# Last w_down forms written in place, M's rows on SP's queue, and four steps of the first half's end put elsewhere

## The chip, the cores and the metric

The kernel runs on one core of one Trainium2 chip. Its time is the device time of one execution, in microseconds (us); what is compared is the median of several executions. The core has five instruction streams that run side by side and wait for each other by semaphores: PE (TensorE, matrix products), ACT (ScalarE), DVE (VectorE), POOL (GpSimd) and SP (SyncE). SP computes nothing here and only starts DMA transfers; POOL starts the others. Each of these two streams starts its transfers in the order of its program, and a transfer that must wait for data holds up all that stand behind it in the same stream.

## The reference

```python
x = A_x                                         # 1 x 2048 x 640
g = sigmoid((x * gate_w).sum(-1, keepdims=True))
# a: linear attention, 32 heads of 20
q, k, v = split(x @ wqkv);  pq, pk = phi(q), phi(k)   # phi(t) = (t+1 if t>0 else exp(t)) + 1e-6
kv = einsum("bhsd,bhse->bhde", pk, v);  z = pk.sum(over s)
a = (einsum("bhqd,bhde->bhqe", pq, kv) / (pq . z + 1e-6)) @ wo
# b: GLU, F = 1536
b = (sigmoid(x @ w_gate) * (x @ w_up)) @ w_down
out = g * a + (1 - g) * b
```

All data are fp32.

## The kernel before

**Products.** `mm3` (L406) makes every product of three matmuls, high by high, high by low and low by high: L407, L408 and L409 in the profile's rows. `split` (L437) makes the two parts of an operand: ACT copies it to the reduced type (the high part, L420), and DVE subtracts that copy from the operand (the low part, L424). Large products are done in a 2 by 2 block form that needs fewer block products and more sums and differences of blocks. Tiles called `xah`, `xrh`, `xbh`, `xth`, `b12h` (and `..l` for low) are parts of such combinations of x's blocks; `w`, `wg`, `wu`, `ws`, `wf`, `wd`, `ds` hold weights and combinations of weights; `cc`, `ch`, `dd`, `rot` are names of PSUM buffers, used in turn.

**Stages.** The positions are worked on in two halves, `pr` = 1 first and then 0.
- The K stage (about 4.6 to 145 us) makes k and phi(k) in four chunks and, in batches, `gt`, the product of phi(k) and x. In its loop over chunks (c = 1 to 3, L1080) a table says after which of a block's steps `s1` to `s5` a piece of work called "qw" is run. At c = 3 "qw" is what `queue_ls` (L743) queued: the sums of w_down's blocks for the last pair of F blocks in the tile `qraw` (DVE, in place), and four `form` calls that split them into tiles `qp` and store these in DRAM (`wd_dram`, stores `wd<-qp`). After the loop the pools that hold `qraw` and `qp` are closed, and the tile `xz` (new positions of x, 5 and 3 rows of blocks, two loads `xz<-xt`) lies over the same memory: its loads wait until the stores have read their tiles.
- `q_phase(1)`, `f_phase(1)` and `last_pair(1)` (145 to 406 us): q, the GLU's blocks in pairs, and for each pair `down_pair`, the product with w_down. The result is summed into `tb`. `last_pair` runs the last of these. In `down_pair` the names are PSUM sums: `W`, `X0`, `X1` are new products; a seed (`V`, `Y0`, `Y1`, `R0`, `U0` and so on) is a copy on ACT of one PSUM sum into another buffer, where more products are added; `out` adds a finished sum to `tb` on DVE. The sigmoid of the pair's last block is `tail[4]` (ACT, the row `cx<-cx`).
- `last_stores` holds two stores of 640 KB, `wd<-wd` on POOL: forms of w_down that the second half loads again.
- `q_phase(0)`, `f_phase(0)`, `last_pair(0)` (406 to 660 us): the same for the second half, with most forms loaded again from DRAM. Beside them the denominators and factors of a are worked out, and `load_ms` (L2463) loads raw rows of the matrix M (the heads' kv times wo, `m_dram`) into the tile `mt`: 8 loads, of 80 KB each. A second call loads 8 others into `mr` and `mv`. `load_m` loads the already split M (`mp_dram`) into `ws` and `wf`.
- The A stage (660 to 725 us): phi(q) times M, scaled, added to b's part and stored. `mt` is first read by DVE here.

**What sets the order.** The class `Order` plans while the program is written: it estimates when PE, ACT and DVE will reach each instruction, holds small pieces of work in a list and writes one when it fits ahead of PE (`fill`), when it is due (`need`, as `order.need((nx[1], 2))`) or at a named place (`run("qw")`). `Ring` estimates the two DMA streams, `sp` and `gp` (SP and POOL), and these estimates decide some of the order too. So a step that is moved by hand can also move pieces that the diff doesn't touch. A hook such as `{7: [queue_scaled]}` runs a function after that step of a phase.

Of the kernel before, what the change touches and what calls it, by code (L numbers as in the profile page):

```python
# [8 lines left out]
F32R = mybir.dt.float32r  # L9
# [5 lines left out]
P = 128  # L15
S, D, F = 2048, 640, 1536
# [14 lines left out]
class Order:  # L31
# [267 lines left out]
    def seed(self, out, at):  # L299
        if out is not None and out.tensor._space == PSUM:  # L300
            self.seeded[out.tensor.name] = at
# [73 lines left out]
def gated_mix_kernel(ctx: ExitStack, tc: tile.TileContext, xt, xn, wk, wv, wo, wst_q, wst_f, out_t):  # L375
# [6 lines left out]
    order = Order()  # L382
    rings = Rings()
    sp, gp = Ring(nc.sync, order, rings, 0, 0.38, 1.5), Ring(nc.gpsimd, order, rings, 1, 0.55, 2.2)

    def f32(ap):
        return ap.bitcast(F32)
# [49 lines left out]
    def split(hi, lo, src, after=""):  # L437
        act(hi, src, AF.Copy, after)
        at = order.act + A_LAG

        def low():
            order.vec = max(order.vec, at)
            vec2(lo, src, f32(hi), OP.subtract)
        order.then(low)
# [295 lines left out]
    qs = qs_cm.__enter__()  # L740
    w_dram, wd_dram = {}, {}

    def queue_ls():  # L743

        p, w = FC // 2 - 1, 4 * P
        wd_dram[p] = dram.tile([P, 2, WF], F32, name=f"wd{p}")
        raw = qs.tile([P, 2, D], F32, name="qraw", tag="qraw")[:, :, :w]
        for j in range(2):
            sp.dma_start(raw[:, j], wst_f[2 * p + j, :, 2, :w])
        (a11, a21), (a12, a22) = [raw[:, j].rearrange("p (q h c) -> h p q c", q=2, h=2) for j in range(2)]  # L750

        def sums(part):
            if part == 0:
                add(a22, a21, a22)
                sub(a21, a11, a21)
            else:
                sub(a11, a22, a11)
                sub(a12, a12, a11)

        def form(j, q):  # L760
            cs = slice(j * w + 2 * q * P, j * w + 2 * (q + 1) * P)
            t = qs.tile([P, 2, 2 * P], F32R, name="qp", tag="qp", bufs=2)
            split(t[:, 0], t[:, 1], raw[:, j, 2 * q * P:2 * (q + 1) * P])
            order.then(lambda: gp.dma_start(wd_dram[p][:, :, 2 * D + cs.start:2 * D + cs.stop], f32(t)))
        for part in range(2):
            order.add(0, 2 * v_cost(2 * P), lambda part=part: sums(part), "qw", None, kept=True)
        for j in range(2):
            for q in range(2):
                order.add(a_cost(2 * P), v_cost(2 * P), lambda j=j, q=q: form(j, q), "qw", None, kept=True)
# [249 lines left out]
    c0 = chunks[0]  # L1019
# [61 lines left out]
    for c in range(1, 4):  # L1081
# [4 lines left out]
        for n in range(1, 6):  # L1086
            order.need((ck, n))
            if c == 1 and n >= 3:
                order.need(("ks", (1, 0, 2)[n - 3]))
            getattr(a, f"s{n}")()  # L1090
            getattr(b, f"s{n}")()
            for _ in range(({1: 1, 2: 1, 3: 1, 5: 1}, {3: 2, 4: 1, 5: 1})[c - 2].get(n, 0) if c > 1 else 0):
                order.run("qw")
        order.need((ck, 6))
        if c == 1:
# [495 lines left out]
    last_stores = []  # L1591
# [102 lines left out]
    c_h, c_l = {}, {}  # L1694
# [9 lines left out]
    def m_rows(dst, cols, queue, u=None):  # L1704

        for d in range(4):
            m = m_dram.rearrange("(h u d) n -> d h u n", u=KC, d=4)[d]
            queue.dma_start(dst[d * H:(d + 1) * H], m[:, u] if cols is None else m[:, :, cols])
# [177 lines left out]
    def down_pair(pr, p):  # L1886
# [22 lines left out]
        def seed(key, tag, src, borrow=False):  # L1909
            ps[key] = (ps_borrow if borrow else ps_tile)(tag)  # L1910
            act(ps[key], ps[src], AF.Copy, "p")
# [13 lines left out]
        def out(key, o, g):  # L1925
            dst = tb[:, o, g]
            if (p, o, g) in FAR[pr]:
                far(key, o, g)
                return
            if (pr, o, g) not in seen:  # L1930
                seen.add((pr, o, g))
                act(dst, ps[key], AF.Copy, "p")
            else:
                add(dst, ps[key], dst, "p")
            order.fill()
# [4 lines left out]
        if p == FC // 2 - 1:  # L1940
            tags = ("cc", "ch") if pr else ("ch", "ch")
            new("W", "dd", "w0", "B11")
            new("X0", tags[0], "A11", "B11")
            seed("V", "dd", "W")
            yield
            new("X1", "ch", "A11", "B11", 1)
            seed("Y0", "rot", "X0")
            seed("Y1", "rot", "X1")
            yield
            def zs():  # L1950
                new("Z0", "ch" if pr else "cc", "S1", "T1")
                out("Z0", 1, 1)
                new("Z1", "cc", "S1", "T1", 1)
                out("Z1", 3, 1)
            if not pr:
                zs()
            go("V", "w1", "B21")
            out("V", 4, 0)
            go("Y0", "A12", "B21")
            out("Y0", 0, 0)  # L1960
            go("Y1", "A12", "B21", q=1)
            out("Y1", 2, 0)
            go("W", "w0", "T1")
            if pr:
                zs()
                go("W", "w1", "B22")
                out("W", 4, 1)
            for q in range(2):
                go(f"X{q}", "S2", "T2", q=q)
                if pr:  # L1970
                    seed(f"R{q}", "rot", f"X{q}")
                out(f"X{q}", 2 * q, 1)
            for q in range(2):
                go(f"Z{q}", "S4", "B22", q=q)
                out(f"Z{q}", 2 * q, 1)
            for q in range(2):
                x = f"R{q}" if pr else f"X{q}"
                go(x, "S3", "T3", q=q)
                seed(f"U{q}", tags[q] if pr else "rot", x)
                out(x, 2 * q + 1, 1)  # L1980
            if pr:
                order.need((nx[1], 2))
                order.need(("wg", ("q", 0, 4)))
            else:
                go("W", "w1", "B22")
                out("W", 4, 1)
            go("U0", "A22", "T4")
            out("U0", 1, 0)
            go("U1", "A22", "T4", q=1)
            out("U1", 3, 0)  # L1990
            return
# [364 lines left out]
            order.add(a_cost(w), v_cost(w), lambda t=t: c.form(t), (nx[1], k))  # L2356
        queue_q(4)
    last_pair(1, tail, next_x)
    for fn in last_stores:
        fn()  # L2360
    q = q_phase(0, lambda k: [(c_h[c][:, k], c_l[c][:, k]) for c in range(2)], {7: [queue_scaled]})

    groups = (2, 3, 0, 1)
    PL, PQ, BL, OMG, MHL = {}, {}, {}, {}, {}
# [98 lines left out]
    def load_ms(i):  # L2463

        if i == 0:
            t = f32(down_pool[1].tile([P, 2, D], F32R, name="mt", tag="mt"))
            raw = [t[:, j] for j in range(2)]
        else:
            raw = [down_pool[1].tile([P, D], F32, name=n, tag=n) for n in ("mr", "mv")]
        for j in range(2):  # L2470
            c0 = (2 * i + j) * P
            m_rows(raw[j].rearrange("p (k c) -> p k c", c=P), slice(c0, c0 + P), gp)
        MR[i] = raw, lambda: max(order.when(t) for t in raw)

    def queue_ms(i):
# [322 lines left out]
```

## Time and profile before

| | before |
|---|---|
| median of 3 runs (lowest, highest) | 731.48 us (730.54, 734.29) |
| the profiled execution | 731.15 us |
| its span in the trace | 729.4 us |
| DVE, ACT, POOL busy | 573.3, 369.7, 106.5 us (79%, 51%, 15%) |
| DMA queues of SP and POOL, share of the 16 engines' span | 49.2%, 26.3% |
| moved | 182.99 MB |

The span runs from the first to the last event that the profiler recorded on the core; the profiled execution's own time is 1.75 us longer. A row of a timeline gives the start and the duration in us, the engine, the line, the operation, the tiles (out<-in), their sizes and, in brackets, how long the engine had been idle and what ended that. Matmuls are pipelined: they start more closely than their durations say, so that their starts, not their ends, show whether PE was held up.

### The profile page before, as it was taken

The page shows a single profiled execution, that of the slowest core. Times are in us where ns is not written, and L with a number is a line of the kernel's source. Part 1 is how long each engine was busy: PE and PEld are TensorE (multiplying, and loading weights), DVE is VectorE, ACT ScalarE, POOL GpSimd, SP SyncE. Part 2 cuts the span into 40 slices and gives each one's busy share as a digit, 9 for nine tenths or more (in the row PEclk, how much of TensorE's full clock was granted, in tenths as well). Part 3 has the DMA queues.
Part 4 walks back from the last instruction along what each step waited for, and adds up shares of the span by engine and source line. Part 5 has one row for each costly group of instructions (what it writes and reads, how often), then busy time and mean ns, then how long its engine had stood idle before and what let it go on. Part 6 is the DMA issues. An engine that isn't in the chain of part 4 may idle for free.

```text
span 729.4 us, 10205 instructions
## 1 busy us (share of the span) xinstructions
PE 723.2 (99%) x3557; PEld 619.2 (85%) x3557; DVE 573.3 (79%) x1008; ACT 369.7 (51%) x686; POOL 106.5 (15%) x173
## 2 busy tenths in 40 slices
PE   9999999999999999999999999999999999999998
PEld 8999999888888888888888888888888888878886
DVE  6888878897777889898989954457585868598896
ACT  6884648357556653535454753454333232443551
POOL 0211113013221211111210123001000003012000
PEclk9999999999999999999999999999999999999999
DMA  7677687898787866457787979879889694969612
GB/s 248 168 227 181 182 210 168 240 322 290 271 301 255 331 240 239 171 223 257 248 329 264 315 236 382 333 241 316 258 271 360 208 339 148 324 232 282 255 65 102
DMA packets 78090, 182.99 MB, mean 251 GB/s; under 512 B 12202, under 2 KB 37818, under 8 KB 74454
## 3 DMA queue, kind: packets, MB, share of 16 engines
q1 hardware_dynamic: 59430, 116.28, 49.2%
q0 software_dynamic: 18464, 65.88, 26.3%
q8 instruction: 28, 0.46, 0.2%
q14 instruction: 24, 0.20, 0.1%
q10 hardware_dynamic: 144, 0.16, 0.1%
HBM read 108.68 MB, written 67.07 MB: 241 GB/s over the span
## 4 chain that ended last, share of the span: by engine, by line
PE 89%; DMA 5%; DVE 3%; ACT 2%; issue 1%; SPq 0%
PE ch L407 10%; PE ch L409 10%; PE ch L408 10%; PE cc L407 8%; PE cc L409 8%; PE cc L408 8%; PE dd L407 7%; PE dd L409 7%; PE dd L408 7%; PE rot L407 5%; PE rot L409 5%; PE rot L408 5%; DMA pl<-p_dram 2%; DMA xz<-xt 1%; DMA wg<-wq 1%; DMA wg<-wd 1%
## 5 line engine op out<-in xcount | busy, mean ns | idle before, releaser
L420 ACT ACTIVATE c<-ch 128x512 f32<-128x512 f32 x52 | 31.1, 598 | 83.7 <-PE ch L409 83.6
L424 DVE TENSOR_TENSOR hf<-c,hf 128x512 fp32r<-128x512 f32 x80 | 54.5, 688 | 23.7 <-ACT hf L420 23.2
L420 ACT ACTIVATE hf<-c 128x512 fp32r<-128x512 f32 x80 | 49.0, 625 | 33.8 <-DVE c L424 33.8
L424 DVE TENSOR_TENSOR c<-cc,c 128x512 f32<-128x512 f32 x40 | 27.6, 689 | 36.8 <-PE cc L409 23.1
L407 PE MATMUL ch<-xth,ws 128*128 128x512 f32 x112 | 43.7, 390 | 0.0
L408 PE MATMUL ch<-xtl,ws 128*128 128x512 f32 x112 | 43.6, 389 | 0.0
L409 PE MATMUL ch<-xth,ws 128*128 128x512 f32 x112 | 43.6, 389 | 0.0
L424 DVE TENSOR_TENSOR tb<-rot,tb 128x512 f32<-128x512 f32 (+1 forms) x58 | 37.3, 676 | 3.0 <-PE rot L409 3.0
L424 DVE TENSOR_TENSOR c<-c,c 128x512 f32<-128x512 f32 x52 | 35.8, 688 | 3.3 <-ACT c L420 2.7
L407 PE MATMUL dd<-xrh,wg 128*128 128x512 f32 x90 | 35.3, 392 | 1.3 <-DVE gt L424 1.3
L409 PE MATMUL dd<-xrh,wg 128*128 128x512 f32 x90 | 35.1, 390 | 0.0
L408 PE MATMUL dd<-xrl,wg 128*128 128x512 f32 x90 | 35.0, 389 | 0.0
L420 ACT ACTIVATE c<-dd 128x512 f32<-128x512 f32 x22 | 13.2, 598 | 41.8 <-PE dd L409 41.8
L407 PE MATMUL cc<-xbh,ws 128*128 128x512 f32 x84 | 32.7, 389 | 0.0
L408 PE MATMUL cc<-xbl,ws 128*128 128x512 f32 x84 | 32.7, 389 | 0.0
L409 PE MATMUL cc<-xbh,ws 128*128 128x512 f32 x84 | 32.7, 389 | 0.0
L424 DVE TENSOR_TENSOR tb<-dd,tb 128x512 f32<-128x512 f32 x36 | 24.7, 687 | 6.6 <-PE dd L409 6.5
L420 ACT ACTIVATE dd<-ch 128x512 f32<-128x512 f32 x22 | 12.8, 582 | 33.6 <-PE ch L409 33.6
L424 DVE TENSOR_TENSOR wst<-wst 128x256 f32<-128x256 f32 (+1 forms) x65 | 24.7, 396 | 1.4
L424 DVE TENSOR_TENSOR tb<-cc,tb 128x512 f32<-128x512 f32 x36 | 24.6, 687 | 1.2 <-PE cc L409 1.2
L409 PEld LDWEIGHTS ch<-xth,ws 128*128 128x128 f32 x112 | 21.0, 188 | 4.7 <-DVE ws L424 0.3
L408 PEld LDWEIGHTS ch<-xtl,ws 128*128 128x128 f32 x112 | 21.0, 188 | 4.3
(663 smaller groups left out, 2371.2 us busy)
## 6 DMA issues: line engine op xcount, KB each, us to landing
wf<-ws POOLq DMA_DIRECT2D x12, 1152.0 KB, 7.6
ws<-wf SPq DMA_DIRECT2D x11, 1152.0 KB, 8.2
wst<-wst_f SPq DMA_DIRECT2D x12, 640.0 KB, 5.3
wf<-wg POOLq DMA_DIRECT2D x12, 640.0 KB, 6.3
wd<-wd POOLq DMA_DIRECT2D x12, 640.0 KB, 8.1
wg<-wf SPq DMA_DIRECT2D x12, 640.0 KB, 6.1
wf<-wd SPq DMA_DIRECT2D x10, 640.0 KB, 10.6
xnst<-xn SPq DMA_DIRECT2D x16, 320.0 KB, 5.0
```

The source lines that it names most:

```text
L407: nc.tensor.matmul(out, l_hi, r_hi, start=first, stop=False, skip_group_check=True)
L408: nc.tensor.matmul(out, l_hi, r_lo, start=False, stop=False, skip_group_check=True)
L409: nc.tensor.matmul(out, l_lo, r_hi, start=False, stop=last, skip_group_check=True)
L420: nc.scalar.activation(out, src, fn, **kw)
L424: nc.vector.tensor_tensor(out, a, b, op=op)
```

## The change

- **w_down's last forms** (`queue_ls`). The high parts of the two `form` calls of one j share one tile `qp`; the low parts are written over the raw sums in `qraw`. Each j stores both with two stores of 128x512 after its second call, where before each call stored a pair of 256 columns.
- **The table of the K stage's loop** at c = 3: two forms after `s4` and two after `s5`, where one and one ran there and the other two at the end.
- **down_pair of the last pair, pr = 1**: the seed `Y0` stands ahead of the product `X1`, which in the program puts it ahead of `tail[4]` and its sigmoid. The product `Z1` by `S4` and its `out` stand behind both `S3` products and behind the need of `(nx[1], 2)`.
- **last_stores** run after step 2 of `q_phase(0)` and not ahead of it.
- **load_ms**: the first call's 8 loads go to `sp`, those of the second call stay on `gp`.

```diff
--- before.py
+++ after.py
@@ -757,11 +757,17 @@
                 sub(a11, a22, a11)
                 sub(a12, a12, a11)
 
+        high = {}
+
         def form(j, q):
-            cs = slice(j * w + 2 * q * P, j * w + 2 * (q + 1) * P)
-            t = qs.tile([P, 2, 2 * P], F32R, name="qp", tag="qp", bufs=2)
-            split(t[:, 0], t[:, 1], raw[:, j, 2 * q * P:2 * (q + 1) * P])
-            order.then(lambda: gp.dma_start(wd_dram[p][:, :, 2 * D + cs.start:2 * D + cs.stop], f32(t)))
+            if q == 0:
+                high[j] = qs.tile([P, 2, 2 * P], F32R, name="qp", tag="qp", bufs=2)
+            src = raw[:, j, 2 * q * P:2 * (q + 1) * P]
+            split(high[j][:, q], src.bitcast(F32R), src)
+            if q:
+                cs = slice(2 * D + j * w, 2 * D + (j + 1) * w)
+                order.then(lambda: [gp.dma_start(wd_dram[p][:, i, cs], t) for i, t in
+                                    enumerate((f32(high[j]).rearrange("p q c -> p (q c)"), raw[:, j]))])
         for part in range(2):
             order.add(0, 2 * v_cost(2 * P), lambda part=part: sums(part), "qw", None, kept=True)
         for j in range(2):
@@ -1089,7 +1095,7 @@
                 order.need(("ks", (1, 0, 2)[n - 3]))
             getattr(a, f"s{n}")()
             getattr(b, f"s{n}")()
-            for _ in range(({1: 1, 2: 1, 3: 1, 5: 1}, {3: 2, 4: 1, 5: 1})[c - 2].get(n, 0) if c > 1 else 0):
+            for _ in range(({1: 1, 2: 1, 3: 1, 5: 1}, {3: 2, 4: 2, 5: 2})[c - 2].get(n, 0) if c > 1 else 0):
                 order.run("qw")
         order.need((ck, 6))
         if c == 1:
@@ -1942,9 +1948,12 @@
             new("W", "dd", "w0", "B11")
             new("X0", tags[0], "A11", "B11")
             seed("V", "dd", "W")
+            if pr:
+                seed("Y0", "rot", "X0")
             yield
             new("X1", "ch", "A11", "B11", 1)
-            seed("Y0", "rot", "X0")
+            if not pr:
+                seed("Y0", "rot", "X0")
             seed("Y1", "rot", "X1")
             yield
             def zs():
@@ -1970,9 +1979,12 @@
                 if pr:
                     seed(f"R{q}", "rot", f"X{q}")
                 out(f"X{q}", 2 * q, 1)
-            for q in range(2):
+            def z4(q):
                 go(f"Z{q}", "S4", "B22", q=q)
                 out(f"Z{q}", 2 * q, 1)
+            z4(0)
+            if not pr:
+                z4(1)
             for q in range(2):
                 x = f"R{q}" if pr else f"X{q}"
                 go(x, "S3", "T3", q=q)
@@ -1980,6 +1992,7 @@
                 out(x, 2 * q + 1, 1)
             if pr:
                 order.need((nx[1], 2))
+                z4(1)
                 order.need(("wg", ("q", 0, 4)))
             else:
                 go("W", "w1", "B22")
@@ -2356,9 +2369,7 @@
             order.add(a_cost(w), v_cost(w), lambda t=t: c.form(t), (nx[1], k))
         queue_q(4)
     last_pair(1, tail, next_x)
-    for fn in last_stores:
-        fn()
-    q = q_phase(0, lambda k: [(c_h[c][:, k], c_l[c][:, k]) for c in range(2)], {7: [queue_scaled]})
+    q = q_phase(0, lambda k: [(c_h[c][:, k], c_l[c][:, k]) for c in range(2)], {2: last_stores, 7: [queue_scaled]})
 
     groups = (2, 3, 0, 1)
     PL, PQ, BL, OMG, MHL = {}, {}, {}, {}, {}
@@ -2469,7 +2480,7 @@
             raw = [down_pool[1].tile([P, D], F32, name=n, tag=n) for n in ("mr", "mv")]
         for j in range(2):
             c0 = (2 * i + j) * P
-            m_rows(raw[j].rearrange("p (k c) -> p k c", c=P), slice(c0, c0 + P), gp)
+            m_rows(raw[j].rearrange("p (k c) -> p k c", c=P), slice(c0, c0 + P), gp if i else sp)
         MR[i] = raw, lambda: max(order.when(t) for t in raw)
 
     def queue_ms(i):
```

POOL's rows at the place of the forms' stores, `wd<-qp`, before: the two stores of each pair have the accumulating stores `zacc<-kr` and `zacc<-kb` of the K stage between and behind them.

```order
L364 DMA zacc<-kb 128x2x320
L364 DMA wd_1295<-qp 256x1x256 x2
L364 DMA zacc<-kr 128x2x320
L364 DMA zacc<-kb 128x2x320
L364 DMA wd_1295<-qp 256x1x256 x2
L364 DMA zacc<-kr 128x2x320
L364 DMA zacc<-kb 128x2x320
```

The same place in the changed kernel:

```order
L364 DMA zacc<-kb 128x2x320
L364 DMA wd_1295<-qp 128x512
L364 DMA wd_1295<-qraw 128x512
L364 DMA wd_1295<-qp 128x512
L364 DMA wd_1295<-qraw 128x512
L364 DMA zacc<-kr 128x2x320
L364 DMA zacc<-kb 128x2x320
```

All four now stand ahead of the `zacc` stores between which the last two stood.

ACT's rows at the start of `last_pair(1)`, before; `dd0<-dd1` is the seed V, `cx<-cx` the sigmoid, `rot0<-cc0` the seed Y0, `rot1<-ch1` the seed Y1, `hf<-cx` the high part of the pair's products.

```order
L420 ACTIVATE dd0_4125<-dd1_4117 128x512
L420 ACTIVATE cx_2339<-cx_2339 128x512
L420 ACTIVATE rot0_4133<-cc0_4121 128x512
L420 ACTIVATE rot1_4135<-ch1_4129 128x512
L420 ACTIVATE hf_4139<-cx_2339 128x512
```

And in the changed kernel:

```order
L420 ACTIVATE dd0_4123<-dd1_4115 128x512
L420 ACTIVATE rot0_4125<-cc0_4119 128x512
L420 ACTIVATE cx_2337<-cx_2337 128x512
L420 ACTIVATE rot1_4133<-ch1_4129 128x512
L420 ACTIVATE hf_4137<-cx_2337 128x512
```

The seed Y0 and the sigmoid have changed places; nothing else has moved there.

SP's rows around M, as a difference (`+` is in the changed kernel alone); `wu<-p_dram` loads phi(q), `pl<-p_dram` phi(q) too.

```order
 L364 DMA wu<-p_dram 128x512
 L364 DMA ws<-mp_dram 128x1920
+L364 DMA mt<-m_dram 32x5x128 x8
 L364 DMA wf<-mp_dram 128x4480
 L364 DMA pl<-p_dram 128x2x512 x2
```

The 8 loads of `mt` now stand on SP, behind `ws<-mp_dram` and ahead of `wf<-mp_dram`; on POOL their place stood ahead of the same stage's accumulating stores `tb<-far`.

## The prediction, written before the changed kernel was run

> **What bounds the kernel now.** I read the page's busy times first.
>
> ```profile
> span 729.4 us, 10205 instructions
> PE 723.2 (99%) x3557; PEld 619.2 (85%) x3557; DVE 573.3 (79%) x1008; ACT 369.7 (51%) x686; POOL 106.5 (15%) x173
> ```
>
> PE is busy for all but 6.2 us, so a change that leaves PE's work as it is can win only where PE stands still. Overlapping records hide short stops, so I went next through PE's timeline and compared starts. In steady work a 512-wide matmul starts 0.23 us after the one ahead (405.08 to 405.31 below), a 320-wide one 0.15 and a 256-wide one 0.12 (estimates from neighbouring starts). A larger distance is a stop. These are the places where it is larger, beside the first 5 us and the last 4 us of the span, which the change doesn't touch:
>
> ```profile
> 136.54 0.30 PE L409 MATMUL dd<-pkh,xnl 128*128 128x320 f32 x1
> 136.92 0.41 PE L407 MATMUL dd<-pkh,xnh 128*128 128x320 f32 x1
> ...
> 142.58 0.39 PE L409 MATMUL ch<-xah,wg 128*128 128x512 f32 x1
> 144.27 0.47 PE L407 MATMUL dd<-xrh,wg 128*128 128x512 f32 x1 [1.30 <-DVE gt L424]
> ...
> 396.82 0.39 PE L409 MATMUL dd<-hf,wd 128*128 128x512 f32 x1
> 397.22 0.50 PE L407 MATMUL rot<-hf,wd 128*128 128x512 f32 x1
> ...
> 405.08 0.39 PE L408 MATMUL rot<-hf,ds 128*128 128x512 f32 x1
> 405.31 0.39 PE L409 MATMUL rot<-hf,ds 128*128 128x512 f32 x1
> 405.69 0.50 PE L407 MATMUL cc<-hf,wd 128*128 128x512 f32 x1
> ...
> 417.37 0.28 PE L409 MATMUL rot<-b12h,wg 128*128 128x256 f32 x1
> 417.70 0.50 PE L407 MATMUL ch<-xah,wg 128*128 128x512 f32 x1
> ...
> 627.17 0.39 PE L409 MATMUL ch<-xth,ws 128*128 128x512 f32 x1
> 627.60 0.50 PE L407 MATMUL dd<-hf,wf 128*128 128x512 f32 x1
> ...
> 639.12 0.39 PE L409 MATMUL cc<-hf,wf 128*128 128x512 f32 x1
> 639.72 0.50 PE L407 MATMUL rot<-hf,wf 128*128 128x512 f32 x1 [0.22 <-DVE tb L424]
> ```
>
> What one stop costs is the distance, less the usual one, plus what the first matmul behind it takes longer (0.50 where others take 0.39, 0.11). That makes 0.38 - 0.15 + 0.10 = 0.33 (136.92); 1.69 - 0.23 + 0.08 = 1.54 (144.27); 0.40 - 0.23 + 0.11 = 0.28 (397.22); 0.38 - 0.23 + 0.11 = 0.26 (405.69); 0.33 - 0.12 + 0.11 = 0.32 (417.70); 0.43 - 0.23 + 0.11 = 0.31 (627.60); 0.60 - 0.23 + 0.11 = 0.48 (639.72). The sum, **3.52 us or 0.48% of the span**, is the most that the change can win. All five parts of it aim at these places, each at one or two.
>
> **Part 1: the last w_down forms (stops at 136.92 and 144.27).** Both stops end when DVE has added `gt<-dd`. The next view was the chain of DVE, ACT and the two DMA streams ahead of it.
>
> ```profile
> 110.42 0.42 DVE L424 TENSOR_TENSOR qp<-qraw,qp 128x256 fp32r<-128x256 f32 x1
> 117.10 0.76 DVE L424 TENSOR_TENSOR qp<-qraw,qp 128x256 fp32r<-128x256 f32 x2
> 119.87 1.95 POOL L364 DMA_DIRECT2D wd<-qp  x2
> SPq L364 <- DMA wd<-qp: 10.7, 1, 10.7
> 125.08 0.98 SPq L364 DMA_DIRECT2D xz<-xt  x2
> 130.32 0.85 ACT L420 ACTIVATE xrh<-xz 128x768 fp32r<-128x768 f32 x1 [4.29 <-DMA xz<-xt]
> 131.20 0.96 DVE L424 TENSOR_TENSOR xrl<-xz,xrh 128x768 fp32r<-128x768 f32 x1 [0.19 <-ACT xrh L420]
> 134.30 0.96 DVE L424 TENSOR_TENSOR xbl<-xz,xbh 128x768 fp32r<-128x768 f32 x1 [1.74 <-ACT xbh L420]
> 142.24 0.69 DVE L424 TENSOR_TENSOR xtl<-xst,xth 128x512 fp32r<-128x512 f32 x1
> ```
>
> The last two forms run at 117.10, their stores start at 119.87, and SP waits 10.7 us for them before the loads of `xz` may overwrite the tiles; ACT then waits 4.29 us for the first of the two loads, and DVE 0.19 and 1.74 us for ACT. From 134.30 on DVE works nearly without a gap up to the late `gt<-dd`. In the change all four forms run by `s5`, where before has the second of them (110.42), and all stores stand ahead of the two `zacc` stores between which the last two stood. I put the last of them at 112, and its landing 5 us later (before, the last took 119.87 to 125.08, 5.2 us), so that SP starts `xz` at about 117 and not 125.08. The loads took 5.2 and 8.3 us until ACT could use them (125.08 to 130.32, and to 134.30 less a copy of 0.85 on ACT), which makes 122 and 125.5, both ahead of the 126.0 at which ACT began to wait (130.32 - 4.29). DVE's two waits go: 0.19 + 1.74 = 1.93 us. The two forms at 117.10 (0.76 us) move ahead, into a stretch where DVE still waits for others; between nothing and 0.76 of it is won, and I take half, 0.38. Against this, DVE's new order has one more subtraction `xtl<-xst` ahead of `gt<-dd`, 0.69 us by the row at 142.24. Net, `gt<-dd` comes 1.93 + 0.38 - 0.69 = **1.62 us earlier**, out of 1.87 that the two stops cost; from both ends 1.24 to 1.87. What is late next is the same DVE chain, by a quarter of a microsecond. The cost of the four in-place subtractions is that of the old ones, since their shapes stay; the two stores per j move the same bytes.
>
> **Part 2: seed Y0 ahead of the sigmoid, Z1 behind S3 (397.22, 405.69).**
>
> ```profile
> 396.05 0.64 ACT L420 ACTIVATE cx<-cx 128x512 f32<-128x512 f32 x1 [0.37 <-DVE cx L424]
> 403.59 0.68 DVE L424 TENSOR_TENSOR tb<-cc,tb 128x512 f32<-128x512 f32 x1
> 405.05 0.58 ACT L420 ACTIVATE cc<-rot 128x512 f32<-128x512 f32 x1 [1.40 <-PE rot L409]
> ```
>
> ACT starts the sigmoid at 396.05, having stood idle for 0.37 us; the seed behind it reaches PE at 397.22, 0.28 late. In the change ACT does the seed in that idle time and just behind it, done by about 396.5, ahead of the 397.05 at which PE would go on (396.82 + 0.23): **0.28 won**. The sigmoid starts some 0.3 later, and with it the DVE product and the split of the pair's last block; PE needs these only some products on, so I cost it at nothing; without that cover it is 0.3. At 405.69 PE waits for the seed U0, copied after the last S3 product at 405.05. The change puts the three matmuls of Z1, 3 x 0.23 = 0.69 us, between; that covers the 0.26. But U0's buffer `cc` is Z0's or Z1's, which DVE must have added first: the row at 403.59 would come to about 404.6 with three matmuls later on PE, close to the seed's 405.05. I take **0.20**, with -0.1 and 0.26 as ends.
>
> **Part 3: last_stores behind step 2 of q_phase(0) (417.70).** PE waits there for `wg<-wq`, a load of 640 KB, in the chain of work that ended last.
>
> ```profile
> 402.66 1.80 POOL L364 DMA_DIRECT2D wd<-wd  x2
> 416.90 0.56 POOL L364 DMA_DIRECT2D p_dram<-qe  x1 [12.44 <-DVE qe L428]
> 410.81 6.84 DMA wg<-wq
> DMA to landing us min/median/max: 4.6/4.6/4.6
> ```
>
> The first row is the two stores, 1.28 MB, the second POOL's next transfer; the last is the next such load in the same stretch (421 us), behind them: 4.6 us, 2.2 us less. In the change the stores stand behind that transfer, so that they start when the load is through (at 4.6 us it lands at 415.4), and the stop goes: **0.32**. The stores then run against loads of f_phase(0), whose weights PE needs later than q_phase(0)'s; I cost that at nothing, and at 0.3 (this stop, moved) if it isn't covered.
>
> **Part 4: M's rows on SP (627.60, 639.72).**
>
> ```profile
> 615.37 4.60 POOL L364 DMA_DIRECT2D mt<-m_dram  x8
> DMA packets 1785, 3.75 MB, mean 297 GB/s; under 512 B 265, under 2 KB 905, under 8 KB 1657
> wf<-wd SPq DMA_DIRECT2D x2, 640.0 KB, 12.0
> 632.98 0.69 DVE L428 SCALAR_TENSOR_TENSOR pl<-pl,fac 128x512 f32<-128x512 f32 x1 [3.49 <-DMA pl<-p_dram]
> 634.39 0.36 SPq L364 DMA_DIRECT2D ws<-mp_dram  x1
> 646.20 0.32 SPq L364 DMA_DIRECT2D wf<-mp_dram  x1
> 660.74 0.84 PE L2600 MATMUL cc<-pq,wf 128*128 128x512 f32 x3
> ```
>
> From 615.37 the 8 loads of `mt` share the engines with `wf<-wd` (12.0 us a load; PE waits at 627.60) and `pl<-p_dram` (DVE waits 3.49 us for it, up to 632.98, and its chain reaches PE 0.48 late at 639.72). The second row is the DMA view of 615 to 627.6 us: 3.75 MB in 12.6 us. Behind `ws<-mp_dram`, at about 634.8, `mt`'s 0.64 MB (17% of that) leave this stretch: at the same 297 GB/s everything there lands 0.64 / 297 = 2.2 us earlier. The first stop is 0.31, the second shows after 3.49 us of DVE's wait of which 2.2 go: both are covered, **0.31 + 0.48**. Behind it on SP stands `wf<-mp_dram`, which started only at 646.20, 11 us after; 8 issues of 0.32 (that row) to 0.58 us (4.60 / 8) are 2.6 to 4.6 us and fit.
>
> The Trainium skill speaks against this part: its page "DMA: Bandwidth & Descriptors", section "Issuing engines are not separate DMA queues", says that transfers started by SyncE, ScalarE or GpSimd run on the same 16 engines and interleave whichever started them, and that another issuer saves only the sequencer's time. By that alone part 4 would win nothing. The trace agrees that they share: `mt` on POOL and `wf<-wd` on SP lie in one stretch of the DMA view. What the page doesn't rule out is that the place in SP's order moves the bytes in time, here by some 19 us.
>
> **The sum.** 1.62 + 0.28 + 0.20 + 0.32 + 0.31 + 0.48 = 3.21 us. The profiled execution's own 731.15 becomes 727.94; the median shown is 0.33 above that execution, so I forecast **728.3**.
>
> **The rivals.**
> - *Part 1 wins nothing* (the stores land no earlier, or DVE's queue is the bound by itself): 728.3 + 1.6 = 729.9. For it speaks DVE's nearly gapless work from 134.30 up to the late `gt<-dd`; against, the 10.7 us on SP. Chance 0.13.
> - *Part 4 wins nothing* (the loads interleave elsewhere with as much harm, or `pl` stays late): 728.3 + 0.8 = 729.1. For it speaks that only the order on SP, and no wait, keeps `mt` from running beside other loads; against, the 11 us up to 646.20 in which SP starts nothing. Chance 0.11. This is the result that the section of the Trainium skill named above would give.
> - *New short stops* take back what is won: four forms in two steps where ACT and DVE feed `kb` and `gt` (two forms more, 0.76 us on each engine), the sigmoid 0.3 late, the stores against f_phase(0)'s loads, and planner moves (`wf<-wd` now ahead of `fac<-fac_dram` on SP): at 3 us together 731.3. Chance 0.08.
> - *Slower*: SP is held by `mt`. If the first load waits until T, `wf<-mp_dram` starts at T + 4.6 and lands perhaps 9 later (an estimate: three quarters of the 12.0 of `wf<-wd` with others beside it), that is T - 647 behind PE's need at 660.74. With 3.2 won elsewhere it is slower by over 0.5% (3.7 us) from T = 654 on, about 735.3. Against it: POOL started the same loads at 615.37. Chance 0.05.
> - The forecast keeps 0.63.
>
> **How the numbers follow.** A measurement of this kernel tells 0.5%, 3.66 us, from no change: below 727.8 is faster. All stops together (3.52) would give 728.0, so a faster verdict needs a stop that I don't see, or the spread of the medians (the runs lie 0.9 below to 2.8 above theirs): a third of the forecast's case and a little of the others, 0.24. Slower is 0.05, and within 0.5% the rest, 0.71. The range goes from 728.0 less 0.9, 727.1, to above the first two rivals, 730.6; the new stops and the slow case lie outside.
>
> **What would show it.** The stops in PE's starts, one by one: none at `gt<-dd` in the K stage or one of 0.3 us, SP's start of `xz<-xt` near 117, no ACT wait on `xz`; PE going from `dd<-hf,wd` to `rot<-hf,wd` without a stop; `wg<-wq` in 4.6 us; `pl<-p_dram` there for DVE near 631, and `mt` after 634. A new stop in PE's timeline, above all at 105 to 115 us or ahead of the A stage, would make the prediction wrong, and so would `xz` later than 122.

## The result, and the profile after

| | before | after |
|---|---|---|
| median of 6 runs (lowest, highest) | 731.58 us (730.54, 734.29) | 727.84 us (727.55, 728.33) |
| the profiled execution, its span | 731.15, 729.4 us | 727.55, 725.8 us |

The changed kernel is faster by 3.74 us, 0.51%; the ratio is 0.9945 with a 95% interval of 0.9929 to 0.9961. The forecast was 728.3 us in a range of 727.1 to 730.6. The page of the changed kernel, its span, busy times and the shares of the chain that ended last by engine:

```profile
span 725.8 us, 10201 instructions
PE 721.5 (99%) x3557; PEld 619.8 (85%) x3557; DVE 573.7 (79%) x1008; ACT 369.0 (51%) x686; POOL 101.2 (14%) x165
PE 99%; DVE 0%; issue 0%
```

The same line of the chain on the page of the kernel before:

```profile
PE 89%; DMA 5%; DVE 3%; ACT 2%; issue 1%; SPq 0%
```

Almost nothing but PE is left in the chain. The 5% of DMA were `pl<-p_dram` (2%), `xz<-xt`, `wg<-wq` and `wg<-wd` (1% each); a part of the change was to free each of the first three, and the fourth is the load that stands ahead of `pl<-p_dram` in SP's chain at 611.95 us. PE's timeline of the changed kernel at the places of the old stops, in the prediction's order (start, duration, engine, line, tiles):

```profile
142.33 0.39 PE L409 MATMUL ch<-xah,wg 128*128 128x512 f32 x1
142.56 0.39 PE L407 MATMUL dd<-xrh,wg 128*128 128x512 f32 x1
...
394.82 0.39 PE L409 MATMUL dd<-hf,wd 128*128 128x512 f32 x1
395.04 0.39 PE L407 MATMUL rot<-hf,wd 128*128 128x512 f32 x1
...
403.15 0.40 PE L409 MATMUL cc<-hf,ds 128*128 128x512 f32 x1
403.39 0.42 PE L407 MATMUL cc<-hf,wd 128*128 128x512 f32 x1
...
415.09 0.28 PE L409 MATMUL rot<-b12h,wg 128*128 128x256 f32 x1
415.21 0.40 PE L407 MATMUL ch<-xah,wg 128*128 128x512 f32 x1
...
624.50 0.39 PE L409 MATMUL ch<-xth,ws 128*128 128x512 f32 x1
624.73 0.39 PE L407 MATMUL dd<-hf,wf 128*128 128x512 f32 x1
...
636.06 0.39 PE L409 MATMUL cc<-hf,wf 128*128 128x512 f32 x1
636.29 0.39 PE L407 MATMUL rot<-hf,wf 128*128 128x512 f32 x1
```

Every pair is 0.22 to 0.24 us apart (0.12 behind a 256-wide one): the stops are gone. The first one is gone too, since nothing between 135 and 138 us is more than 0.2 us apart.

Other rows of the changed kernel's timelines, of POOL, SP, ACT and DVE in the K stage:

```profile
111.55 0.54 POOL L364 DMA_DIRECT2D wd<-qraw  x1
116.46 1.61 SPq L364 DMA_DIRECT2D xz<-xt  x2
125.70 0.83 ACT L420 ACTIVATE xrh<-xz 128x768 fp32r<-128x768 f32 x1
141.09 0.68 DVE L424 TENSOR_TENSOR xtl<-xst,xth 128x512 fp32r<-128x512 f32 x1
141.70 0.88 DVE L424 TENSOR_TENSOR gt<-dd,gt 128x320 f32<-128x320 f32 x2
```

The last store starts at 111.55, SP starts `xz` at 116.46 and not at 125.08, ACT waits for neither load, and `gt<-dd` starts at 141.70 and not at 143.63. The one subtraction `xtl` that the new order puts ahead of it stands there as forecast.

Two new holds came. Rows of PE's weight loads (PEld), PE and ACT near 401 us, and of the weight loads near 412 us:

```profile
401.19 0.19 PEld L407 LDWEIGHTS rot<-hf,ds 128*128 128x128 f32 x1 [0.24 <-ACT rot L420]
401.22 0.48 PE L407 MATMUL rot<-hf,ds 128*128 128x512 f32 x1
401.53 0.40 PE L408 MATMUL rot<-hf,ds 128*128 128x512 f32 x1
399.01 0.63 ACT L420 ACTIVATE hf<-cx 128x512 fp32r<-128x512 f32 x1 [0.92 <-DVE cx L424]
400.55 0.59 ACT L420 ACTIVATE rot<-cc 128x512 f32<-128x512 f32 x1
411.82 0.19 PEld L408 LDWEIGHTS rot<-xbl,wg 128*128 128x128 f32 x1 [0.22 <-DVE xbl L424]
```

The seed R0 (`rot<-cc`) is ready just as PE comes. PE's matmul starts in time, but lasts 0.48, and the next starts 0.31 and not 0.23 us later; some twenty behind it keep 0.23 to 0.24 where they had 0.227. Together that is 0.23 us: by so much PE's way from here to 406.88 us is longer than in e5 below, which has no hold here. ACT makes the seed at the end of a row of work without a gap, from `hf<-cx` on, which waited for DVE and, through it, for the sigmoid. At 411.82 the weight load for `xbl` waits 0.22 us for DVE, which costs PE 0.09. No row of PE itself names a wait at either place.

The DMA rows of the stretch at 613 to 625.6 us, SP's timeline behind it, and the longest of SP's own waits between 628 and 638.6 us (us in total, times, longest):

```profile
DMA packets 2154, 4.56 MB, mean 362 GB/s; under 512 B 212, under 2 KB 968, under 8 KB 2026
wf<-wd SPq DMA_DIRECT2D x2, 640.0 KB, 7.4
627.96 10.50 SPq L364 DMA_DIRECT2D mt<-m_dram  x8
642.60 0.33 SPq L364 DMA_DIRECT2D wf<-mp_dram  x1
SPq L364 <- DMA ws<-mp_dram: 3.6, 1, 3.6
```

Without M's rows `wf<-wd` takes 7.4 and not 12.0 us, and the stretch moves 362 and not 297 GB/s. The 8 issues on SP take 10.5 us, more than twice what was forecast, 3.6 of them a wait for one older transfer to land, and still end 4 us ahead of `wf<-mp_dram`. They also start at 627.96 and not at about 634.8, the place in SP's order that the prediction gave them.

### The profile page after: what moved, and what is told of

Its sections match the earlier page's. It is cut to its first block, busy times and chain, and to the rows that moved or that the text cites. A ratio compares the mean times of both kernels' runs of the same rounds, so it can differ in the third digit from the quotient of the medians.

```text
span 725.8 us, 10201 instructions
## 1 busy us (share of the span) xinstructions
PE 721.5 (99%) x3557; PEld 619.8 (85%) x3557; DVE 573.7 (79%) x1008; ACT 369.0 (51%) x686; POOL 101.2 (14%) x165
## 4 chain that ended last, share of the span: by engine, by line
PE 99%; DVE 0%; issue 0%
PE ch L407 11%; PE ch L408 11%; PE ch L409 11%; PE cc L407 9%; PE cc L408 9%; PE cc L409 9%; PE dd L407 7%; PE dd L408 7%; PE dd L409 7%; PE rot L408 5%; PE rot L407 5%; PE rot L409 5%; PE rot L1549 1%; PE rot L495 0%; PE ch L2611 0%; PE cc L2611 0%
## 5 line engine op out<-in xcount | busy, mean ns | idle before, releaser
L420 ACT ACTIVATE c<-c 128x512 f32<-128x512 f32 x34 | 21.3, 628 | 6.9 <-DVE c L424 6.4
```

Source lines behind the costliest of these rows:

```text
L420: nc.scalar.activation(out, src, fn, **kw)
```

## The experiments

Each group of runs was made beside the kernel before on the same chip. The kernel before alone differs by 1.0 us from group to group, so that medians of different groups aren't compared, and PE's 21st matmul starts anywhere between 6.2 and 7.4 us of the span in these executions, whatever the kernel. So I also worked out from PE's recorded starts how long PE takes from its 21st matmul to its last. That column is of one execution each: between 145 and 393 us, where many of these kernels don't differ, it differs by up to 0.2 us. The profiled execution is the slowest of its runs for e2, e6, e8 and e11 and the fastest for e9 and the changed kernel.

```
kernel                    median  before  ratio, 95%        PE 21st to last, and against after
before                    731.58          1                 719.06  +3.67
after                     727.84  731.58  0.9929 to 0.9961  715.39
e1_forms_old              730.16  732.17  0.9967 to 0.9987  717.30  +1.91
e2_table_old              729.44  732.17  0.9945 to 0.9973  717.13  +1.74
e7_old_forms_new_table    731.78  732.17  0.9986 to 1.0012  719.11  +3.73
e10_low_twice             728.72  732.17  0.9934 to 0.9971  716.31  +0.93
e3_ms_pool                729.80  732.57  0.9952 to 0.9978  717.59  +2.21
e8_ms_pool_late           731.87  732.57  0.9984 to 1.0005  720.21  +4.82
e4_stores_early           728.76  732.57  0.9940 to 0.9969  715.84  +0.46
e5_y0_late                727.98  732.57  0.9929 to 0.9959  715.45  +0.06
e6_z1_early               728.09  732.28  0.9925 to 0.9955  716.01  +0.63
e9_forms_alone            730.26  732.28  0.9956 to 0.9980  716.81  +1.42
e11_ms_alone              730.64  732.28  0.9961 to 0.9981  718.45  +3.06
e12_whole_rows            728.07  732.28  0.9927 to 0.9957  715.49  +0.11
```

### e1: part 1 undone

```diff
-for _ in range(({1: 1, 2: 1, 3: 1, 5: 1}, {3: 2, 4: 2, 5: 2})[c - 2]...
+for _ in range(({1: 1, 2: 1, 3: 1, 5: 1}, {3: 2, 4: 1, 5: 1})[c - 2]...
...
-split(high[j][:, q], src.bitcast(F32R), src)
+t = qs.tile([P, 2, 2 * P], F32R, name="qp", tag="qp", bufs=2)
+split(t[:, 0], t[:, 1], raw[:, j, 2 * q * P:2 * (q + 1) * P])
```

> The changed kernel with part 1 undone: the old forms of w_down and the old table of the K stage, all else as changed. Theory (each part removes its own stops of PE, and the parts add up): the two stops at gt<-dd come back near 136.9 and 144.2 us of the span, 1.87 us together, SP starts xz<-xt near 125, and the time is 727.8 + 1.9 = 729.7 us. Rival (the gain of part 1 is partly the planner's reordering behind it, or part of another part's gain): a time that is off that by more than 0.5 us, 728.5 or 730.5.

PE's way is 1.91 us longer, the theory's 1.87. Both stops are back (1.78 us at their two places, the rest spread behind them); PE and SP show the second and its cause:

```profile
144.89 0.47 PE L407 MATMUL dd<-xrh,wg 128*128 128x512 f32 x1 [1.30 <-DVE gt L424]
125.68 0.97 SPq L364 DMA_DIRECT2D xz<-xt  x2
```

### e2: only the table undone

```diff
-{3: 2, 4: 2, 5: 2}
+{3: 2, 4: 1, 5: 1}
```

> The changed kernel with only the old table of the K stage at c = 3 (two forms by s5, two at the end); the forms share buffers and are stored in two pieces per j as in the change. Theory (what counts is when the last store lands, because SP waits for it before xz<-xt): the second j's forms run near 116 to 117, their stores start near 118, SP waits some 9 us for them, and both stops come back in full: 729.6 us. Rival (fewer, larger stores land earlier by themselves, so that the form of the stores does the work): SP starts xz<-xt before 121, at most half of the stops comes back, 728.7 or less.

POOL's, SP's and PE's rows:

```profile
120.22 1.04 POOL L364 DMA_DIRECT2D wd<-qp  x1
125.09 0.97 SPq L364 DMA_DIRECT2D xz<-xt  x2
144.39 0.47 PE L407 MATMUL dd<-xrh,wg 128*128 128x512 f32 x1 [1.30 <-DVE gt L424]
```

The stores in their new form start at 120.22 and SP is held until 125.09, as before (119.87, 125.08). The large stop is back in full, the small one is not: 1.74 us. The form of the stores does almost nothing by itself (0.17 us, the distance to e1); when the last one lands decides.

### e7: only the forms undone

The table of the change stays, and the old `form` of e1's diff comes back.

> The changed kernel with the old forms (each with its own tile qp out of two buffers, one store each) under the new table, four forms by s5. Theory (the shared buffers are what allows four forms by s5): the third form must wait until the first form's store has read its tile; the store starts near 108.9 and needs about 4 to 5 us, so ACT stands until about 113.5 with the work of the K stage behind the form, some 3 us, and PE gets a new stop of 1 to 3 us near 110 to 116: 729 to 731 us. Rival (the table alone does it): no wait on ACT over 0.5 us, no stop, 727.8 us.

ACT's and PE's rows:

```profile
112.90 0.42 ACT L420 ACTIVATE qp<-qraw 128x256 fp32r<-128x256 f32 x1 [2.42 <-DMA wd<-qp]
114.10 0.42 ACT L420 ACTIVATE qp<-qraw 128x256 fp32r<-128x256 f32 x1 [0.79 <-DMA wd<-qp]
119.60 0.41 PE L408 MATMUL rot<-pkl,xnh 128*128 128x320 f32 x1 [0.56 <-DVE pkl L428]
```

Its windows (the stretch, then its length, then busy time and instructions of PE, PEld, DVE, ACT and POOL, the granted clock of PE, the DMA share and GB/s):

```profile
119.00:121.90 2.90, 1.85 (x8) 1.09 (x8) 2.77 (x6) 2.59 (x6) 0.00 (x0) 1.00 0.98 227
121.90:125.20 3.30, 3.30 (x14) 3.30 (x14) 1.79 (x5) 2.69 (x5) 0.03 (x1) 0.52 1.12 318
```

ACT waits 2.42 and 0.79 us for the first stores to let go of the two buffers. PE gets the new stop, not at 110 to 116 but from 118.7 on, where the work behind the forms is used, and it is dearer than expected, 3.73 us: behind the stops the granted clock is 0.52 for 3.3 us, in which 12 matmuls start 0.267 and not 0.147 us apart, 1.4 us in all. All of the gain of the change is lost. So the shared buffers are not a saving in themselves: they are what lets the table move the forms.

### e10: how much room is left

```diff
             split(*self.f.b_part(k0, k1, self.cs), self.x[1][:, k0:k1])
+            if self.b12 and self.pr and self.c:
+                hi, lo = self.f.b_part(k0, k1, self.cs)
+                order.then(lambda: nc.vector.tensor_tensor(lo, self.x[1][:, k0:k1], f32(hi), op=OP.subtract))
```

> The changed kernel with one subtraction on DVE written twice, xbl<-xz of 128x768 near 131.6 us of the span (0.86 us from start to start), with the same result. It measures how much room is left ahead of the place where PE stood for gt<-dd. In the changed kernel the first of the two gt<-dd ends at 142.18, and the matmul that waits for it starts at 142.56: room of 0.2 to 0.4 us. Theory (DVE's chain is the next bound there, just covered): a stop of 0.5 to 0.8 us comes back near 142.5, the time is 728.3 to 728.6. Rival (DVE has slack of over 0.9 us, since planned pieces can wait): no stop, 727.8.

PE's row:

```profile
133.97 0.41 PE L407 MATMUL rot<-pkh,xnh 128*128 128x320 f32 x1 [0.56 <-DVE gt L424]
```

An operation of 0.86 us costs 0.93. The stop isn't at 142.5 but already at 133.97, at another sum of `gt`, so the room that I read at 142.5 was the wrong place's. There PE comes 0.71 us late for 0.86 more on DVE, so that DVE's chain has at most 0.15 of room; it is the next bound, as the prediction had it, though nothing of it shows in the profile of the changed kernel.

### e3: M's rows back on POOL

```diff
-slice(c0, c0 + P), gp if i else sp)
+slice(c0, c0 + P), gp)
```

> The changed kernel with the 8 loads of M's rows back on POOL, all else as changed. Theory (they share the DMA engines with wf<-wd and pl<-p_dram): POOL starts them near 612, PE's two stops come back near 624 and 636 us of the span, 0.31 and 0.48 us, and the time is 727.8 + 0.8 = 728.6 us. Rival (the moves of the other parts, which start this stretch 3 us earlier, already cleared it): at most one short stop, under 0.3 us, 728.0.

PE's rows, and the DMA view of 613.2 to 626.1 us:

```profile
626.15 0.50 PE L407 MATMUL dd<-hf,wf 128*128 128x512 f32 x1 [0.85 <-DMA wf<-wd]
638.63 0.50 PE L407 MATMUL rot<-hf,wf 128*128 128x512 f32 x1 [0.22 <-DVE tb L424]
DMA packets 1699, 3.54 MB, mean 274 GB/s; under 512 B 264, under 2 KB 900, under 8 KB 1571
wf<-wd SPq DMA_DIRECT2D x2, 640.0 KB, 12.7
```

The stops are back, and cost 2.2 us and not 0.8. `wf<-wd` took 12.7 us here and 12.0 in the profile of the kernel before. PE asks for it 11.8 us after its start (627.40 less 615.57 there), so that some tenths of landing go straight to PE, and a late DVE adds a second and third stop.

### e11: M's rows on SP, alone

The same line, in the kernel before.

> The kernel before with part 4 alone (M's rows on SP). Theory: wf<-wd takes about 7.5 us and not 12.0, both stops at 627 and 640 go, 0.8 us below the profile of the kernel before; since the same loads on POOL cost 2.2 us in the changed kernel (a landing 0.7 us later at the same place), the gain against the median of the kernel before may be 0.8 to 2.2 us, and its runs lie closer together. Rival (part 4 needs the others, or SP is held too long by the 8 loads, 10.5 us in the changed kernel): no gain or a stop ahead of the A stage at 660 us, 731 us or more.

```profile
wf<-wd SPq DMA_DIRECT2D x2, 640.0 KB, 8.4
```

Both stops are gone, and PE's way is 0.61 us shorter; a stop at `wg<-wq` was 0.28 us longer in this execution, without which it would be the 0.9 that the two stops cost by PE's starts. In medians it is 1.64 us of 732.28. Ten runs lie within 1.2 us (730.14 to 731.32), where 19 of the kernel before beside them spread over 3.4 and ten of e9 over 2.5.

### e9: part 1, alone

Part 1's diff, in the kernel before.

> The kernel before with part 1 alone (w_down's forms and the table). Theory (the parts are separate places and add up): PE's end 1.9 us earlier than before, counted from PE's 20th matmul, the stops at 397, 405, 418, 627 and 640 as they were, less 1.9 us; 1.9 us below the kernel before of the same chip. Rival (the later stops swallow or enlarge it): a gain outside 1.5 to 2.3.

```profile
wf<-wd SPq DMA_DIRECT2D x2, 640.0 KB, 11.3
```

PE's way is 2.25 us shorter than before. `wf<-wd` took 11.3 us in this execution, the fastest of its ten, with M's rows on POOL, and the stop of 0.31 us at it is absent: 1.87 of part 1 and that. In medians it is 2.02 us, within the theory's bounds.

### e8: M's rows on POOL, but later

```diff
-        (FC - 1, 4): [lambda: load_ms(0), a_first],
+        (FC - 1, 4): [a_first],
...
     queue_lo()
+    load_ms(0)
     load_ms(1)
```

with e3's line. 

> The changed kernel with the same 8 loads on POOL, but called for after the last pair of the second half, so that they stand behind the stores tb<-far (near 650 us of the span). The planner then also puts some pieces of the A stage in another order. Theory (what counts is when the bytes move, not which queue starts them): no stop near 624 or 636, PE's end within 0.1 us of the changed kernel's, 727.8 us. Rival (POOL's queue as such disturbs SP's loads, or SP's order is what helps): a stop of 0.3 us or more in 620 to 640, or a new one behind 650 where these loads now run beside others, 728.3 or more.

Between 604 and 690 us PE's starts keep the same distance from the changed kernel's to 0.01 us: POOL's queue does no harm there, so what matters is when the bytes move. The time is lost behind 650 us, where the rival had these loads run beside others, at stops from 691 on. PE's first stop and the DVE rows ahead of it, then the DVE row of the same work in the changed kernel:

```profile
692.35 0.50 PE L408 MATMUL cc<-pq,ws 128*128 128x512 f32 x1 [0.44 <-DVE pq L424]
676.62 1.30 DVE L428 SCALAR_TENSOR_TENSOR hf<-hf,fac 128x512 f32<-128x512 f32 x2 [6.02 <-DMA hf<-p_dram]
684.37 0.70 DVE L424 TENSOR_TENSOR cc<-tb,omg 128x512 f32<-128x512 f32 x1 [3.95 <-DMA omg<-gate_dram]
```

```profile
672.25 6.00 DVE L428 SCALAR_TENSOR_TENSOR hf<-hf,fac 128x512 f32<-128x512 f32 x9 [3.22 <-DMA hf<-p_dram]
```

The first stop stands at an operand that isn't made from M's rows, but DVE reaches it late: it waits 6.02 us for `hf<-p_dram` on SP, whose loads take 17.0 and 19.5 us (two sizes) beside M's rows on POOL, where the changed kernel has 14.6 and 15.7, and then 3.95 for `omg<-gate_dram` (1.37 in the changed kernel). By these rows the late loads do at 652 to 680 us what they did at 615. The planner had also put pieces of the A stage in another order, so that their share of the 4.6 us isn't separated.

### e12: whole rows in place of short pieces

```diff
+            for d in range(4):
+                rows = slice(d * H, (d + 1) * H)
+                gp.dma_start(raw[j][rows], wst_f[0, rows, j])
```

> The changed kernel with M's 8 loads on POOL as in the run with them put back, but each of 32 whole rows of 2560 bytes of a weight and not 160 pieces of 512 bytes of M: the same bytes, a fifth of the pieces; part of the output is then wrong, since M's rows aren't loaded. Theory A (what they cost the other loads is their number of pieces): wf<-wd takes at most 10 us (7.4 without them, 12.7 with M's pieces), and at most one stop of 0.3 us is left near 624 to 638. Theory B (their bytes): wf<-wd takes 12 us or more, and the stops are those of M's pieces, 1.8 to 2.2 us together.

The DMA view of 613 to 624.4 us:

```profile
DMA packets 1508, 3.37 MB, mean 296 GB/s; under 512 B 254, under 2 KB 764, under 8 KB 1380
wf<-wd SPq DMA_DIRECT2D x2, 640.0 KB, 11.3
```

Neither theory holds. 11.3 us is more than A allows and less than B does; it is what e9 shows with M's short pieces, and the rate, 296 GB/s, is that of the kernel before (297). But the edit changed less than it was meant to: by the trace POOL moved M's rows in 256 data packets (1024 and 4096 bytes) and moves the whole rows in 128 (5120 bytes). Half the packets don't lift the rate; a fifth was not tested. That no stop is left (+0.11) is a matter of 11.3 lying below the 11.8 that PE gives it.

### e4: last_stores ahead of q_phase(0) again

```diff
+    for fn in last_stores:
+        fn()
-... {2: last_stores, 7: [queue_scaled]})
+... {7: [queue_scaled]})
```

> The changed kernel with last_stores back ahead of q_phase(0). Theory: wg<-wq takes near 6.8 us again instead of the changed kernel's, PE's stop of 0.32 us comes back near 415, 728.1 us. The orders that the planner changed in the second half (denominators' loads and factors on SP, DVE and POOL) go back to those of the kernel before with it, and the theory gives them nothing. Rival (these orders are worth something): PE's starts differ from the changed kernel's by another 0.1 us or more between 430 and 610.

```profile
416.21 0.50 PE L407 MATMUL ch<-xah,wg 128*128 128x512 f32 x1
```

PE's row comes 0.36 behind the one ahead of it (415.85), 0.12 being usual; PE's distance to the changed kernel grows by 0.33 at this place and stays there to the end. The planner's new orders in the second half are worth nothing. The other 0.13 of the 0.46 lies ahead of 397 us, where the kernels don't differ: so much do executions differ by themselves.

### e5 and e6: the two moves of part 2

e5:

```diff
-            if pr:
-                seed("Y0", "rot", "X0")
             yield
             new("X1", "ch", "A11", "B11", 1)
-            if not pr:
-                seed("Y0", "rot", "X0")
+            seed("Y0", "rot", "X0")
```

> The changed kernel with the seed Y0 behind X1 and the sigmoid again. Theory: PE's stop of 0.28 us comes back near 394.6, 728.1 us, and the place of Z1 later on loses nothing. Rival (the earlier stages' 1.9 us changed what ACT waits for, so the sigmoid no longer stands in the way): no stop, 727.8 us.

e6:

```diff
             z4(0)
-            if not pr:
-                z4(1)
+            z4(1)
...
                 order.need((nx[1], 2))
-                z4(1)
```

> The changed kernel with Z1's last product back ahead of the S3 products; the seed Y0 stays early. What is to be told: how part 2's gain is shared. In the changed kernel and in every run so far with Y0 early, PE has no stop at the seed Y0 but is held for about 0.30 us at the seed R0 (near 401 us), which the run with Y0 late doesn't show; with Z1 late there is no stop at U0. First theory (each move removes its own stop): the stop at U0 of 0.26 us comes back and nothing else, 728.1 us. Second theory (Y0's move only carries the stop on to R0, and all that is won is Z1's): the way from 393 to 414 us is as long as in the kernel before, 20.5 us against 20.2 in the changed one, with a hold at R0 and a stop at U0; 728.1 us too, so that PE's starts decide.

PE's rows, first of e5, then of e6:

```profile
396.02 0.50 PE L407 MATMUL rot<-hf,wd 128*128 128x512 f32 x1
```

```profile
403.92 0.50 PE L407 MATMUL cc<-hf,wd 128*128 128x512 f32 x1
407.36 0.50 PE L408 MATMUL dd<-xrl,wg 128*128 128x512 f32 x1 [0.16 <-DVE xrl L424]
```

With Y0 late its stop is back (396.02 is 0.40 behind the row ahead, 395.62), but the hold at R0 is gone, and the sum is +0.06. With Z1 early the stop at U0 is back (0.26), a stop at `xrl` follows (0.43; DVE now does Z1's `out` ahead of it), and there is no hold at R0 either. PE's way over the stretch from 393 to 414 us (its 2091st to 2179th matmul) is 20.51 us before, 20.21 after, 20.16 with Z1 late alone (e5) and 20.63 with Y0 early alone (e6). Neither theory of e6 is right: the hold needs both moves. Counted from PE's 2091st matmul, the early Y0 makes the sigmoid start at 0.70 and not at 0.38 us, and ACT's `hf<-cx`, from which on ACT works without a gap up to R0, at 5.33 and not at 5.03 (the changed kernel and e5). Z1's three matmuls were 0.68 us of cover for that, which the other move takes away. With Y0 late the seed is made 0.17 earlier and PE comes 0.27 later. The hold at `xbl` is in neither run: PE comes there 0.15 (e5) and 0.72 us (e6) later.

## Why the prediction came out as it did

- **What bounds the kernel.** Right. The gain is in the main the sum of stops (3.67 us of PE's way, 3.74 in the medians; the sum of the seven was 3.52, and 3.21 was forecast), and all seven are gone. By PE's starts the seven places, with the two new holds, give 3.4; the other 0.25 lies between them in steps of at most 0.03, such as executions of equal code show too. That 3.67 comes so near to 3.52 is in part luck.
- **Part 1.** Mechanism right and shown by e1, e2 and e7: the last store's landing holds SP, and early forms need the shared buffers. The term was mis-sized, 1.62 for 1.87 to 1.91: `gt<-dd` came 1.93 us earlier by the timelines, and not 1.62. By DVE's rows 0.24 of that lies ahead of 121 us, where the moved forms were (put at 0.38), and 1.69 behind it: the waits that went are worth 2.3 start to start and not 1.93, and the one more subtraction costs 0.60 and not 0.69. That DVE's chain is next is shown by e10, which leaves it at most 0.15.
- **Part 2.** The sum of 0.48 was too high, 0.30 by PE's way. The step that failed is "PE needs these only some products on, so I cost it at nothing": the seed R0 stands on ACT behind the work that the sigmoid starts, which came 0.30 later, and it lost its cover when Z1's matmuls went from ahead of it. 0.23 came at R0 and 0.09 at `xbl`, together the 0.3 that the text gives for the case without cover. The doubt about U0's buffer was right too: ACT's copy at 402.68 waits for DVE's `tb`, and PE's matmul at 403.39 finds it barely ready (0.42 long, the next start 0.255 and not 0.227 later). Z1's move alone is worth 0.35, Y0's move nothing on top of it (-0.05, within what executions differ by).
- **Part 3.** Right: 0.32 forecast, 0.33 by e4. `wg<-wf` behind it now takes 6.5 us beside the stores, where it took 4.6, and no stop comes of it.
- **Part 4.** Right in sign and place; in size nearly, for the profiled execution of before (0.79 forecast, 0.90 by PE's starts). Two steps were off. That "everything there lands 0.64 / 297 = 2.2 us earlier" used the rate with both queues at work; without M's rows it is 362 GB/s, and `wf<-wd` came 4.6 us earlier. And the profile of one execution priced a landing that varies: 11.3, 12.0 and 12.7 us in three executions with M's rows on POOL, with PE's need at 11.8, which makes stops of none, 0.31 and 1.1 us out of the same code. That is why e3 loses 2.2, and I take it for a reason that the median of before lies above the profiled execution; the latter is argued from e11's narrower runs and not shown (e3's five runs, with M's rows on POOL, lie within 1.2 us too). The issue of the 8 loads on SP was put at 2.6 to 4.6 us and took 10.5, because SP waited between them for older transfers; that it did no harm is owed to their early start, 14.6 us ahead of `wf<-mp_dram` and not 11.
- **The rival "part 4 wins nothing"** fell with e3 and e11. What it feared, as much harm elsewhere, came in e8, where the same loads run on POOL at 652 us: PE is as free at 604 to 690 us as in the changed kernel, and held behind that. The Trainium skill's page "DMA: Bandwidth & Descriptors" (section "Issuing engines are not separate DMA queues") was set beside the rival; e8 agrees with the page that transfers share the DMA engines whichever issuer started them, since the loads on POOL make SP's `hf<-p_dram` slower (17.0 for 14.6 us). So part 4 won by the place in time, which that section doesn't speak of.
- **The chances.** The boundary of 0.5% was met almost exactly (0.51%); 0.71 for within it was too sure, given that the stops' sum alone reached 0.48% and that single profile rows had been taken for the price of a varying wait.

## What to carry to other kernels

When PE is busy for 99% of the span, read its starts and not its waits: seven stops of a quarter to one and a half microseconds held all that there was to win, and only two had a wait beside them in their row. A wait at the edge (a load that lands within half a microsecond of its need) has no single price in one profile; look at several executions, and move it well clear. And when a product is moved, ask which later operand it had been covering.

## What was not expected of the hardware

- In one stretch, two DMA queues at work at once moved less than one alone: 274 to 297 GB/s with M's rows (or whole rows of the same bytes) on POOL beside SP's loads, 362 without. Half as many, larger packets made no difference (e12). It is no rule for two queues: from 412 to 416 us of the kernel before POOL moves 1.11 MB and SP 0.53, at 411 GB/s together. Why isn't settled.
- A short hold costs PE more than itself: behind the stops between 512-wide matmuls the first one takes 0.48 to 0.50 us and the next start comes 0.31 to 0.34 later, and ten to twenty behind it run at 0.23 to 0.24 and not 0.227 us. At R0, where PE's weight load waited 0.24 us and PE itself not at all, that came to 0.23 us.
- In e7 the clock fell to about half (0.52) for 3.3 us after 3.2 us in which PE stood in four stops, the longest start to start 0.94 us. The Trainium skill's page "TensorE: Matmul & The Clock Gate" ("Part 1: The HAM clock gate") has the clock halve after at least one idle window of about 3.4 us; here PE worked in between, so a stretch that is only partly idle was enough. The seven stops of the kernel before, each alone, left the clock at 1.00.
- The start of PE's 21st matmul varied by 1.1 us between executions, and the landing of the first loads is the smaller part of it: the first matmul on loaded data starts between 4.27 and 4.67 us in all of them. The clock is the larger. In e9 the 12 matmuls up to the 21st take 1.97 us, in e11 2.97, most of them 0.27 us apart and not 0.15; the trace's record of the full clock begins at 3.7 us in e9 and at 6.9 in e11.
